# An attention, expert and routing kernel on one core: products of zeros in its opening made float32, fewer in number, and eight of them in other places

## The chip, the cores and the metric

The kernel runs on 1 core of one Trainium2 chip. The metric is the device time in microseconds (us). Times of single runs of the kernel before are 471.6, 471.64 and 473.65 us, with a median of 471.64. One more execution was profiled, and all rows below come from it.

## The reference

```python
for c in range(nc):                                   # chunks of 32 queries
    k_ctx, v_ctx = keys and values from 16 before the chunk to 8 behind it
    k_full, v_full = 8 memory rows, then k_ctx, v_ctx
    a = softmax(q_c @ k_full.T / sqrt(64))            # 4 batches, 8 heads, 768 positions
    out[c] = a @ v_full
x = out as 3072 tokens of 512
h = x @ w_in ; g = h * sigmoid(h) ; y = g @ w_out     # 512 -> 2048 -> 512
logits = y @ phi                                      # 32 slots: 8 experts of 4
slot_input = softmax(logits over tokens).T @ y
slot_out[e] = relu(slot_input[e] @ w1[e]) @ w2[e]     # 512 -> 1024 -> 512
result = softmax(logits over slots) @ slot_out
```

## The kernel before

The 3072 tokens are 24 groups of 128. Attention is done group by group, and the tokens then go through the first two weight matrices in seven blocks of 256 to 512 tokens. The products of a block with one of the 16 pieces of w_in are what the code calls an h.

The program is written out by hand. The string OPENING lists the work of the opening word by word, and each word is one call, put on its engine's queue in that order; every engine then works through its own queue, and waits there for semaphores alone. The first letter says what is done (the dictionary `ops`), the first number for which group or weight piece, and the last numbers of S, T, V and W are PSUM banks:

- q and v load a group's queries with keys, and its values. w and b load a weight piece, c and d convert it in steps (ACT, then DVE), C and D make its high and its low half, R is a small product with phi.
- S is a group's scores (`a_scores`, L266: 32 float32 products), M and U its maximum and subtraction on DVE, E its exponential on ACT, O and N its sum and inverse on DVE, Q its division (Q.1.p: on POOL).
- T turns a group's probabilities (`a_turn`, L311: four 128x128 transposes), A keeps them (ACT, L186), V multiplies them by the values (`a_values`, L328: 32 float32 products), X and Y are the high and the low half of the result (ACT L186, DVE L382).
- h is a group of products with weights (`emit_h`, L399), s and t its tanh and multiplication.
- W is `keep_warm(n, b)`: n products of zeros into bank b (L182), which nothing reads.

The products of zeros are bfloat16, of 128 columns of zeros with 512 others. The zeros lie in a part of the tile `call` that holds results of the routing later on:

```python
warm = [call[:, 0:8].rearrange("p t s -> p (t s)").bitcast(BF16)]       # L114
nc.vector.memset(call[:, 0:8], 0.0)                                     # L755
keep_warm(10)                                                           # L758
```

Ten stand at the start, and 27 in six places of OPENING: W.12.0 ahead of the scores of group 4, W.2.6 ahead of those of group 3, W.3.7 ahead of the values of group 1, W.4.5 ahead of the turn of group 0, W.3.4 ahead of the values of group 0, and W.3.7 ahead of the values of group 3. The order of the groups in the opening is 2, 1, 0, 4, 3 for the scores and 1, 2, 0, 4, 3 for the turns; the values come as 1, 2, 0, 3, 4. After V.4 follow h.0, h.2 and so on, with no more products of zeros in the opening.

The loads are all issued by SP, in the order of their words. A weight piece (512 KB) is loaded into one of five buffers, and so waits until an earlier piece in it has been converted.

Of the kernel before, what the change touches and what calls it, by code (L numbers as in the profile page):

```python
# [11 lines left out]
BF16 = mybir.dt.bfloat16  # L12
# [12 lines left out]


OPENING = """
q.2 q.1 q.0 S.2.4.5 M.2 U.2 w.1 S.1.6.2 c.1.0 i M.1 U.1 E.1 q.4 S.0.3.7 M.0 W.12.0 S.4.1.0 E.2 O.1 N.1 q.3 W.2.6
S.3.4.5 U.0 w.0 c.1.1 O.2 N.2 E.0 O.0 N.0 v.1 c.0.0 c.0.1 v.0 M.4 U.4 Q.1.p T.1.6 A.1.a v.2 Q.2.p T.2.2 A.2.a W.3.7
V.1.3.7 E.4 Q.0.p W.4.5 T.0.6 c.0.3 C.0 D.0.p b.2 X.1 M.3 U.3 E.3 V.2.2.1 w.2 b.0 A.0.a c.2.0 c.2.1 O.4 N.4 W.3.4  # L30
V.0.0.5 v.3 O.3 N.3 X.2 Q.4.p T.4.4 Y.1 Q.3.p X.0 c.2.3 T.3.6 A.3.a W.3.7 V.3.3.7 v.4 A.4.a c.1.3 C.1 D.1.p b.1
V.4.6.4 d.2.0 Y.2 X.3 w.3 Y.0 h.0 h.2 X.4 Y.3 d.1.0 Y.4 s.0 t.0 h.3 z.0 p d.2.1 d.2.3 v.5 d.1.1 d.1.3 s.2 d.0.0 d.0.1
b.3 t.2 z.2 h.1 C.2 D.2.p w.5 d.0.3 R.0 R.1 R.2 s.3 t.3 z.3 h.4 w.4 c.3.0 c.3.1 c.3.3 s.1 t.1 h.5 z.1 C.3 b.5 c.5.0
c.5.1 c.5.3 s.4 t.4 c.4.0 c.4.1 c.4.3 D.3.p h.7 s.5 t.5 z.5 h.6 b.4 d.3.0 d.3.1 d.3.3 R.3 C.4 D.4.v d.5.0 s.7 t.7 s.6
t.6 z.6 q.5 w.6 S.5.2.5 M.5 U.5 C.5 h.9 e.0 D.5.p d.4.0 d.4.1 c.6.0 c.6.1 c.6.3 w.8 s.9 t.9 z.9 h.10 s.10 t.10 q.6
C.6 D.6.v b.7 P.0.3 F.0 d.4.3 d.5.1 d.5.3 h.8 s.8 t.8 d.7.0 d.7.1 h.13 c.8.0 c.8.1 c.8.3 w.7 s.13 t.13 E.5 O.5 h.12
s.12 t.12 z.12 b.6 C.8 z.4 S.6.4.6 w.9 d.7.3 z.7 R.4 R.5 c.7.0 c.9.0 d.6.0 b.8 N.5 h.11 s.11 D.8.p h.16 z.8 z.10 t.11
z.11 d.6.1 d.6.3 w.10 c.7.1 c.7.3 L.0.0 c.9.1 c.9.3 C.7 L.1.0 s.16 t.16 Q.5.p T.5.5 A.5.a R.6 R.7 c.10.0 d.8.0 d.8.1
q.7 M.6 U.6 h.17 s.17 t.17 b.9 e.1 D.7.p h.14 b.10 C.9 d.8.3 s.14 t.14 z.14 E.6 O.6 N.6 w.12 V.5.5.4 v.6 X.5 c.10.1
c.10.3 S.7.6.7 M.7 d.10.0 d.10.1 q.8 h.15 s.15 t.15 z.15 D.9.p h.18 h.19 C.10 D.10.p Y.5 s.18 w.11 z.17 d.9.0 d.9.1  # L40
d.9.3 c.12.0 c.12.1 P.1.4 F.1 d.10.3 b.13 c.12.3 C.12 Q.6.p T.6.5 U.7 A.6.a L.0.1 L.1.1 E.7 R.8 R.9 R.10 D.12.p
V.6.4.6 s.19 t.18 h.20 O.7 N.7 Q.7.p t.19 z.19 h.21 c.11.0 c.11.1 c.11.3 b.11 d.11.0 w.14 s.20 t.20 h.25 C.11 D.11.p
z.13 c.14.0 b.12 d.12.0 s.21 t.21 z.21 h.23 c.14.1 c.14.3 d.11.1 d.11.3 R.11 X.6 T.7.5 Y.6 w.15 s.25 t.25 z.25 d.13.0
d.13.1 d.13.3 e.2 S.8.4.6 M.8 U.8 s.23 t.23 h.22 C.14 P.2.7 v.7 A.7.a V.7.5.4 d.12.1 d.12.3 s.22 t.22 z.22 q.9 E.8
O.8 N.8 F.2 L.1.2 L.0.2 R.12 z.16 D.14.p h.28 s.28 t.28 z.28 h.29 c.15.0 c.15.1 c.15.3 b.14 d.14.0 d.14.1 d.14.3 C.15
D.15.v b.15 d.15.0 d.15.1 d.15.3 h.31 s.29 t.29 z.29 w.13 c.13.0 c.13.1 c.13.3 s.31 Q.8.p t.31 z.31 h.30 v.8 T.8.6
X.7 Y.7 s.30 t.30 z.30 A.8.a R.13 R.14 R.15 e.3 V.8.4.5 v.9 C.13 D.13.v S.9.6.7 q.10 M.9 U.9 X.8 h.24 s.24 t.24 z.24
h.27 s.27 h.26 z.20 z.18 P.3.6 Y.8 t.27 B.0 F.3 L.1.3 z.27 z.23 E.9 O.9 N.9 s.26 t.26 L.0.3 z.26 Q.9.v
"""


# [1 line left out]
def attn_moe_softmoe_kernel(  # L53
# [13 lines left out]
    nc = tc.nc  # L67
    NB = len(BLOCKS)
    L = NB - 1
# [8 lines left out]
    z = const.tile([128, 10240], F32, name="z")  # L78
# [35 lines left out]
    call = const.tile([128, NT, 32], F32, name="call")  # L114
    acc = const.tile([128, 4, 512], F32, name="acc")
    s_run = const.tile([128, 1], F32, name="s_run")
    warm = [call[:, 0:8].rearrange("p t s -> p (t s)").bitcast(BF16)]

    misc = [[4, 5, 6], 0]

    def bank(b, shape, name):
        if b is None:
            return mbank(shape, name)
        return psum.tile(shape, F32, tag=f"b{b}", name=name)

    def mbank(shape, name):
        misc[1] += 1
        return bank(misc[0][misc[1] % len(misc[0])], shape, name)
# [39 lines left out]
    def load_raw(key):  # L168
        o = 7168 if key[0] == "o" else 1024 * (len(raw_t) % 5)
        raw_t[key] = oarena[:, o:o + 1024].bitcast(U32).rearrange("p (n two) -> p n two", two=2)  # L170
        nc.sync.dma_start(out=raw_t[key], in_={"w": win, "b": woutt, "o": wout}[key[0]][key[1]])
# [7 lines left out]
    def keep_warm(n, b=0):  # L179
        pw = bank(b, [128, 512], "ps_warm")  # L180
        for _ in range(n):
            nc.tensor.matmul(pw, warm[0][:, 0:128], warm[0], start=True, stop=True)  # L182

    def copy(eng, out, in_):
        if eng == "a":
            nc.scalar.activation(out=out, in_=in_, func=ACTF.Copy)  # L186
        else:
            nc.vector.tensor_copy(out=out, in_=in_)
# [8 lines left out]
    def conv(key, s):  # L197
        raw = raw_t[key]
        lo_w, hi_w = raw[:, :, 0], raw[:, :, 1]
        if key not in cx:  # L200
            o = (5120, 5632, 6144, 7168, 7680)[len(cx) % 5]
            cx[key] = oarena[:, o:o + 512]
        x = cx[key]
        xb = x.bitcast(U32)
        if s == 0:
            nc.scalar.activation(out=x, in_=hi_w.bitcast(F32), func=ACTF.Prelu, scale=REBIAS, alpha=-(2.0**32))  # L206
        elif s == 1:
            nc.scalar.activation(  # L208
                out=lo_w, in_=raw.bitcast(U16)[:, :, 1], func=ACTF.Copy, scale=2.0**-13, bias=-4095.75 / 8192
            )  # L210
        elif s == 2:
            return
        else:
            nc.vector.scalar_tensor_tensor(  # L214
                out=xb, in0=xb, scalar=3, in1=lo_w, op0=ALU.logical_shift_left, op1=ALU.bitwise_or
            )
# [535 lines left out]
            at(*WO[u], 1, wo_load, u + 1)  # L752

    with tc.manual_schedule():
        nc.vector.memset(call[:, 0:8], 0.0)  # L755
        nc.vector.memset(s_run, 0.0)
        nc.scalar.activation(out=s_run, in_=s_run, func=ACTF.Exp)
        keep_warm(10)  # L758

        def step(fn):  # L760
            return lambda i, *a: fn(i % 2, i // 2, *a)

        ops = {
            "q": load_qk, "v": load_v, "w": lambda f: load_raw(("w", f)), "b": lambda f: load_raw(("b", f)),
            "i": load_cst, "p": load_phi, "W": keep_warm,
            "c": lambda f, s: conv(("w", f), s), "d": lambda f, s: conv(("b", f), s), "C": conv_hi, "D": conv_lo,
            "R": wp_q, "e": wp_keep, "P": wp_sum, "F": wp_out,
            "S": a_scores, "M": a_max, "U": a_sub, "E": a_exp, "O": a_sum, "N": a_inv, "Q": a_norm,
# [48 lines left out]
        last_sum((2, by))  # L817
        c_keep = c_turn(0, 4, bx, "a")
        keep_warm(3, 4)
        last_max()  # L820
        g_turn(L, NF - 1)
# [15 lines left out]
        for tag in ("lp", "ll"):  # L837
            t = sm_p.tile([128, 512], F32, tag=tag, name="siz", bufs=1)
# [46 lines left out]
        for half in range(2):  # L885
            for cb in range(2):
                for m in (2 * half, 2 * half + 1):
                    for q in range(4):
# [3 lines left out]
                            start=(m == 0), stop=(m == 3), tile_position=(0, 32 * q),  # L892
# [235 lines left out]
```

## Time and profile before

| | |
|---|---|
| median of 3 runs | 471.64 us |
| profiled execution, own time | 471.73 us |
| its span, first to last instruction | 470.0 us |
| mean granted TensorE clock | 0.986 |
| PE busy (products) | 450.1 us, 96% |
| PEld busy (weight loads) | 336.5 us, 72% |
| DVE busy | 343.1 us, 73% |
| ACT busy | 187.2 us, 40% |
| POOL busy | 43.9 us, 9% |
| moved by DMA | 93.68 MB, mean 199 GB/s |

Times in the rows are counted from the first instruction. A row of the timeline merges neighbouring instructions of one line and one pair of operands: start, length, engine, line, operation, tiles, shape and number, and in brackets how long the engine had been idle and what ended that. "issue" there is time in which the engine waited for nothing that the profile shows. PE is TensorE's products, PEld its weight loads, SPq the issuing of loads. Some records of products can be missing, so that a run of 12 may show as 11. A row of stretches has the stretch, its length, and for PE, PEld, DVE, ACT and POOL the busy time and the number of instructions; then PEclk, the share of the full TensorE clock that was granted, the share of the DMA engines' time that was used, and GB/s.

### The profile page before, as it was taken

To read this page: it belongs to the slowest core of one execution; us is meant where nothing else is said; L and a number is where in the kernel's file an instruction comes from. 1 tells how busy PE (TensorE), PEld (TensorE's weight loads), DVE (VectorE), ACT (ScalarE), POOL (GpSimd) and SP (SyncE) were. 2 spreads that over 40 slices of the span, in tenths; PEclk is the share of its full clock that TensorE was granted. 3 is DMA by queue.
4 is the path that set the end of the run, shared out by engine and by line. 5 is a ranking of instruction groups with operands and counts; after the bars stand their busy time and mean duration, and the time that the engine had idled before them with its cause. 6 is when DMAs were issued, how large, how long until landed. Compare 5 with 4: busy or idle time off the path is not lost.

```text
span 470.0 us, 14626 instructions
## 1 busy us (share of the span) xinstructions
PE 450.1 (96%) x6395; PEld 336.5 (72%) x6402; DVE 343.1 (73%) x785; ACT 187.2 (40%) x401; POOL 43.9 (9%) x41
## 2 busy tenths in 40 slices
PE   7699999989999999999999999999999999999992
PEld 4489988979776777677776778677787789643642
DVE  4757788867889998889998699987865764551142
ACT  2468878863342234233343243341343222221132
POOL 0422134300000001000110011100100000000000
PEclk9889999999999999999999999999999999999997
DMA  8947688464111225124442244412314999799988
GB/s 323 396 150 278 246 307 317 165 215 146 54 49 54 99 100 188 46 99 146 144 153 83 93 149 147 144 52 75 101 47 144 404 409 384 285 412 406 400 288 277
DMA packets 30336, 93.68 MB, mean 199 GB/s; under 512 B 2880, under 2 KB 9280, under 8 KB 30272
## 3 DMA queue, kind: packets, MB, share of 16 engines
q1 hardware_dynamic: 30272, 92.74, 53.8%
q8 instruction: 50, 0.82, 0.7%
q14 instruction: 14, 0.11, 0.1%
HBM read 86.44 MB, written 6.29 MB: 197 GB/s over the span
## 4 chain that ended last, share of the span: by engine, by line
PE 84%; DVE 5%; DMA 4%; ACT 2%; issue 2%; SPq 0%; DVEq 0%; ACTq 0%
PE ps_h L399 51%; PE ps_a L579 6%; PE ps_l L446 5%; PE ps_s L266 3%; PE ps_o L960 3%; PE ps_x L352 3%; PE ps_e L926 3%; PE ps_x L328 2%; DMA oarena<-in_win_dram 2%; DMA aarena<-in_qk_dram 1%; PE ps_warm L182 1%; PE ps_f L1009 1%; DVE garena L426 1%; DVE oarena L214 1%; PE ps_t L311 1%
## 5 line engine op out<-in xcount | busy, mean ns | idle before, releaser
L399 PE MATMUL ps_h<-x,w 128*128 128x512 f32 (+2 forms) x704 | 151.6, 359 | 1.5 <-ACT w L186 1.1
L399 PEld LDWEIGHTS ps_h<-x,w 128*128 128x128 f32 x704 | 124.0, 188 | 23.4 <-issue 3.1
L399 PE MATMUL ps_h<-x1a,w 128*128 128x512 f32 (+2 forms) x544 | 139.0, 362 | 0.0
L421 ACT ACTIVATE garena<-ps_h 128x512 f32<-128x512 f32 (+3 forms) x113 | 60.0, 532 | 168.6 <-PE ps_h L399 151.1
L399 PEld LDWEIGHTS ps_h<-x1a,w 128*128 128x128 f32 x544 | 98.9, 188 | 20.0 <-issue 5.0
L426 DVE SCALAR_TENSOR_TENSOR garena<-garena,ps_h 128x512 f32<-128x512 f32 (+3 forms) x113 | 67.8, 601 | 43.2 <-ACT garena L421 42.1
L430 DVE STREAM_TRANSPOSE z<-garena 128x512 f32<-128x512 f32 (+2 forms) x112 | 69.4, 628 | 4.2 <-PE ps_a L579 0.9
L191 POOL TENSOR_TENSOR aarena<-aarena,smm 128x512 f32<-128x512 f32 x19 | 22.7, 1193 | 226.1 <-DVE smm L301 226.1
L214 DVE SCALAR_TENSOR_TENSOR oarena<-oarena 128x512 uint32<-128x512 uint32 x46 | 31.1, 690 | 7.1 <-ACT oarena L208 7.0
L206 ACT ACTIVATE oarena<-oarena 128x512 f32<-128x512 f32 x46 | 30.4, 665 | 12.6 <-DMA oarena<-in_win_dram 11.9
L208 ACT ACTIVATE oarena<-oarena 128x512 uint32<-128x512 uint16 x48 | 31.6, 667 | 0.0
L399 PE MATMUL ps_h<-x1b,w 128*128 128x512 f32 x64 | 25.0, 390 | 0.0
L446 PE MATMUL ps_l<-garena,aarena 128*32 128x512 f32 (+2 forms) x216 | 24.7, 544 | 0.0
L579 PE MATMUL ps_a<-z,d 32*32 32x512 f32 x672 | 23.6, 598 | 0.0
L274 DVE TENSOR_REDUCE mx<-ps_s 128x4 f32<-128x256 f32 x48 | 17.8, 411 | 6.2 <-PE ps_s L266 6.1
L191 POOL TENSOR_TENSOR w<-oarena,w 128x512 fp32r<-128x512 f32 x12 | 15.9, 1321 | 52.1 <-ACT w L186 52.1
L266 PE MATMUL ps_s<-aarena 64*32 64x64 f32 x1280 | 17.2, 224 | 1.1 <-DMA aarena<-in_qk_dram 1.1
L579 PEld LDWEIGHTS ps_a<-z,d 32*32 32x32 f32 x672 | 10.6, 103 | 9.6 <-issue 5.9
L293 ACT ACTIVATE aarena<-aarena 128x512 f32<-128x512 f32 x20 | 12.6, 629 | 7.9 <-DVE aarena L290 5.7
L590 DVE SCALAR_TENSOR_TENSOR acc<-acc,al,ps_a 128x512 f32<-128x512 f32 x20 | 13.9, 742 | 2.5 <-PE ps_a L579 2.4
L266 PEld LDWEIGHTS ps_s<-aarena 64*32 64x32 f32 x1280 | 13.9, 105 | 2.5 <-DMA aarena<-in_qk_dram 1.2
L287 DVE TENSOR_TENSOR aarena<-ps_s,mx 128x256 f32<-128x256 f32 x40 | 14.8, 409 | 0.1
(211 smaller groups left out, 469.6 us busy)
## 6 DMA issues: line engine op xcount, KB each, us to landing
aarena<-in_qk_dram SPq DMA_DIRECT2D x20, 608.0 KB, 5.4
aarena<-in_v_dram SPq DMA_DIRECT2D x20, 512.0 KB, 4.1
oarena<-in_win_dram SPq DMA_DIRECT2D x16, 512.0 KB, 5.2
oarena<-in_woutt_dram SPq DMA_DIRECT2D x16, 512.0 KB, 5.7
oarena<-in_wout_dram SPq DMA_DIRECT2D x16, 512.0 KB, 3.2
w<-in_w_dram SPq DMA_DIRECT2D x16, 512.0 KB, 7.1
z<-in_w_dram SPq DMA_DIRECT2D x9, 512.0 KB, 8.0
oarena<-in_w_dram SPq DMA_DIRECT2D x8, 512.0 KB, 9.3
```

Source lines behind the costliest of these rows:

```text
L191: (nc.gpsimd if eng == "p" else nc.vector).tensor_tensor(**kw)
L206: nc.scalar.activation(out=x, in_=hi_w.bitcast(F32), func=ACTF.Prelu, scale=REBIAS, alpha=-(2.0**32))
L208: nc.scalar.activation(out=lo_w, in_=raw.bitcast(U16)[:, :, 1], func=ACTF.Copy, scale=2.0**-13, bias=-4095.75 / 8192)
L214: nc.vector.scalar_tensor_tensor(out=xb, in0=xb, scalar=3, in1=lo_w, op0=ALU.logical_shift_left, op1=ALU.bitwise_or)
L266: nc.tensor.matmul(ps[r][q, p], t[h, p, q], t[h, p, w:w + 64], start=True, stop=True)
L274: nc.vector.tensor_reduce(out=mx[:, 4 * r:4 * r + 4], in_=ps_t[g][r], axis=AX.X, op=ALU.max)
L399: nc.tensor.matmul(ph, w_t[f][:, wi, 128 * c:128 * c + 128], x[c], start=(c == 0 and m == 0), stop=(c == 3 and m == 2),)
L421: nc.scalar.activation(out=g[:, t], in_=h_t[j, f][:, t], func=ACTF.Tanh, scale=0.5)
L426: nc.vector.scalar_tensor_tensor(out=g[:, t], in0=g[:, t], scalar=1.0, in1=h[:, t], op0=ALU.add, op1=ALU.mult)
L430: nc.vector.transpose(out=z_view(j)[:, slot], in_=g_t[j, f])
L446: nc.tensor.matmul(rt[j, "pl"][32 * m:32 * m + 32], wp[:, f], g_t[j, f], start=(k == ks[0]), stop=(k == ks[-1] or j == L and m > 1 and k = ...
L579: nc.tensor.matmul(ps[q][32 * cg:32 * cg + 32], d[p, t], zv[p, :, t], start=(b < 4), stop=(b >= nb - 4), tile_position=(32 * q, 32 * cg),)
```

## The change

A second helper makes products of zeros in float32. The zeros become twice as many (512 float32 columns; the bfloat16 products still use the first 256). Ten bfloat16 products at the start become two float32 and two bfloat16 ones. In OPENING, W.12.0 becomes Z.3.0 in the same place; W.2.6 ahead of the scores of group 3, W.3.7 ahead of the values of group 1, W.4.5 ahead of the turn of group 0 and W.3.4 ahead of the values of group 0 are gone; Z.2.6 stands ahead of the turn of group 1 and Z.3.4 ahead of the values of group 2. W.3.7 ahead of the values of group 3 stays. The table OPENING is otherwise the same, word for word:

```
before: ... M.0 W.12.0 S.4.1.0 ... q.3 W.2.6 S.3.4.5 ... Q.1.p T.1.6 ... W.3.7 V.1.3.7 E.4 Q.0.p W.4.5 T.0.6 ... E.3 V.2.2.1 ... N.4 W.3.4 V.0.0.5
now:    ... M.0 Z.3.0 S.4.1.0 ... q.3 S.3.4.5 ... Q.1.p Z.2.6 T.1.6 ... V.1.3.7 E.4 Q.0.p T.0.6 ... E.3 Z.3.4 V.2.2.1 ... N.4 V.0.0.5
```

```diff
@@ -114,7 +114,8 @@
     call = const.tile([128, NT, 32], F32, name="call")
     acc = const.tile([128, 4, 512], F32, name="acc")
     s_run = const.tile([128, 1], F32, name="s_run")
-    warm = [call[:, 0:8].rearrange("p t s -> p (t s)").bitcast(BF16)]
+    zeros = call[:, 0:16].rearrange("p t s -> p (t s)")
+    warm = [zeros[:, 0:256].bitcast(BF16)]
 
     misc = [[4, 5, 6], 0]
 
@@ -180,6 +181,11 @@
         pw = bank(b, [128, 512], "ps_warm")
         for _ in range(n):
             nc.tensor.matmul(pw, warm[0][:, 0:128], warm[0], start=True, stop=True)
+
+    def zero_products(n, b):
+        pw = bank(b, [128, 512], "ps_warm")
+        for _ in range(n):
+            nc.tensor.matmul(pw, zeros[:, 0:128], zeros, start=True, stop=True)
 
     def copy(eng, out, in_):
         if eng == "a":
@@ -752,17 +758,18 @@
             at(*WO[u], 1, wo_load, u + 1)
 
     with tc.manual_schedule():
-        nc.vector.memset(call[:, 0:8], 0.0)
+        nc.vector.memset(zeros, 0.0)
         nc.vector.memset(s_run, 0.0)
         nc.scalar.activation(out=s_run, in_=s_run, func=ACTF.Exp)
-        keep_warm(10)
+        zero_products(2, 0)
+        keep_warm(2)
 
         def step(fn):
             return lambda i, *a: fn(i % 2, i // 2, *a)
 
         ops = {
             "q": load_qk, "v": load_v, "w": lambda f: load_raw(("w", f)), "b": lambda f: load_raw(("b", f)),
-            "i": load_cst, "p": load_phi, "W": keep_warm,
+            "i": load_cst, "p": load_phi, "Z": zero_products, "W": keep_warm,
             "c": lambda f, s: conv(("w", f), s), "d": lambda f, s: conv(("b", f), s), "C": conv_hi, "D": conv_lo,
             "R": wp_q, "e": wp_keep, "P": wp_sum, "F": wp_out,
             "S": a_scores, "M": a_max, "U": a_sub, "E": a_exp, "O": a_sum, "N": a_inv, "Q": a_norm,
```

On PE, from the scores of group 3 to the values of group 1, the program stood so before (call holds the zeros, ps_s are scores, ps_t turns, ps_x values; "x32" is 32 instructions of the program, and a float32 product is one row with its weight load in it):

```order
L182 LDWEIGHTS call
L182 MATMUL ps_warm<-call 128x512
L182 LDWEIGHTS call
L182 MATMUL ps_warm<-call 128x512
L266 MATMUL ps_s<-z 32x64 x32
L311 MATMUL ps_t<-cst,z 128x128 x8
L182 LDWEIGHTS call
L182 MATMUL ps_warm<-call 128x512
...
L328 MATMUL ps_x<-z 64x32 x32
```

and stands so now:

```order
L272 MATMUL ps_s<-z 32x64 x32
L188 MATMUL ps_warm<-call 128x512 x2
L317 MATMUL ps_t<-cst,z 128x128 x8
L334 MATMUL ps_x<-z 64x32 x32
```

The two bfloat16 products ahead of the scores are gone, two float32 ones stand between the scores and the eight turns of groups 1 and 2, and the values of group 1 follow the turns with nothing between.

On PE, from the values of group 1 to the turn of group 4, the program stood so before:

```order
L328 MATMUL ps_x<-z 64x32 x32
L182 LDWEIGHTS call
L182 MATMUL ps_warm<-call 128x512
...
L311 MATMUL ps_t<-cst,aarena 128x128 x4
L328 MATMUL ps_x<-z 64x32 x32
L182 LDWEIGHTS call
L182 MATMUL ps_warm<-call 128x512
...
L328 MATMUL ps_x<-aarena 64x32 x32
L311 MATMUL ps_t<-cst,w_332 128x128 x4
```

and stands so now:

```order
L334 MATMUL ps_x<-z 64x32 x32
L317 MATMUL ps_t<-cst,aarena 128x128 x4
L188 MATMUL ps_warm<-call 128x512 x3
L334 MATMUL ps_x<-z 64x32 x32
L334 MATMUL ps_x<-aarena 64x32 x32
L317 MATMUL ps_t<-cst,w_315 128x128 x4
```

The four products ahead of the turn of group 0 and the three ahead of its values are gone; three float32 ones stand between that turn and the values of group 2. On the other engines only the memset of the zeros differs, 128x512 for 128x256.

## Rows read from the trace of the kernel before

**Rows 1.** The page: busy time by engine, and the queue of instructions (packets, MB, share).

```profile
PE 450.1 (96%) x6395; PEld 336.5 (72%) x6402; DVE 343.1 (73%) x785; ACT 187.2 (40%) x401; POOL 43.9 (9%) x41
...
q8 instruction: 50, 0.82, 0.7%
```

**Rows 2.** Timeline of PE, from the start to h.0.

```profile
1.19 4.45 PE L182 MATMUL ps_warm<-call 128*128 128x512 bf16 x10 [1.19 <-DVE s_run L756]
...
8.60 0.86 PE L266 MATMUL ps_s<-aarena 64*32 64x64 f32 x64 [1.08 <-DMA aarena<-in_qk_dram]
...
9.39 2.76 PE L182 MATMUL ps_warm<-call 128*128 128x512 bf16 x11
...
13.12 0.78 PE L266 MATMUL ps_s<-acc 64*32 64x64 f32 x55 [0.60 <-issue]
...
15.15 0.98 PE L311 MATMUL ps_t<-cst,z 128*128 128x128 f32 x7
...
19.17 0.33 PE L311 MATMUL ps_t<-cst,z 128*128 128x128 f32 x1 [3.04 <-issue]
...
20.21 2.06 PE L328 MATMUL ps_x<-z 64*64 64x32 f32 x64
...
30.33 1.15 PE L328 MATMUL ps_x<-z 64*64 64x32 f32 x64
...
32.34 0.38 PE L399 MATMUL ps_h<-x,w 128*128 128x256 f32 x1
```

**Rows 3.** DMA by queue: 10.7-10.9, 16.7-16.8, 22.8-23, 26.4-26.6, 33.6-34.6 us.

```profile
q8 instruction: 1, 0.02, 33.3%
...
q1 hardware_dynamic: 12, 0.04, 103.6%
...
q8 instruction: 1, 0.02, 68.2%
...
q8 instruction: 1, 0.02, 32.1%
...
q8 instruction: 1, 0.02, 27.4%
...
q8 instruction: 1, 0.02, 5.9%
```

**Rows 4.** Three stretches: busy time of each engine, granted clock, DMA share.

```profile
19.00:20.00 1.00, 0.78 (x3) 0.35 (x4) 0.00 (x0) 0.47 (x1) 0.00 (x0) 0.94 1.02 406
20.00:25.00 5.00, 4.78 (x77) 3.38 (x80) 3.31 (x8) 2.37 (x7) 2.46 (x3) 0.50 0.69 271
26.00:27.00 1.00, 0.84 (x33) 0.82 (x31) 0.28 (x1) 0.83 (x3) 0.00 (x0) 0.64 0.05 16
```

**Rows 5.** Chain of waits around the end of h.0: start, us, what.

```profile
34.08 0.40 ACT garena L421
```

**Rows 6.** PE's groups by form: zero products in bfloat16, float32 products (mean ns).

```profile
L182 PE MATMUL ps_warm<-cst 128*128 128x512 bf16 x2 | 0.6, 379 | 0.1
...
L487 PE MATMUL ps_r<-lp,cst 128*128 128x256 f32 x2 | 0.6, 378 | 0.0
```

**Rows 7.** Timeline of DVE, ACT and SP in the opening.

```profile
0.86 0.27 DVE L755 MEMSET call<- 128x256 f32 x1 [0.86 <-PEq L1117]
...
18.00 0.74 DVE L287 TENSOR_TENSOR z<-ps_s,mx 128x256 f32<-128x256 f32 x2
...
22.30 0.66 ACT L186 ACTIVATE x<-ps_x 128x256 fp32r<-128x256 f32 x2 [1.13 <-PE ps_x L328]
...
24.98 0.60 ACT L186 ACTIVATE aarena<-ps_t 128x512 f32<-128x512 f32 x1 [1.50 <-PE ps_t L311]
...
26.72 1.29 DVE L214 SCALAR_TENSOR_TENSOR oarena<-oarena 128x512 uint32<-128x512 uint32 x2 [1.39 <-ACT oarena L208]
...
28.09 0.33 SPq L171 DMA_DIRECT2D oarena<-in_woutt_dram  x1
...
29.68 0.60 ACT L186 ACTIVATE z<-ps_t 128x512 f32<-128x512 f32 x1 [0.35 <-PE ps_t L311]
```

More of the change, by code (lines that the diff above doesn't have):

```diff
@@ L27 @@
 OPENING = """
[L28 to L47, printed above, removed]
@@ L48 @@
-h.27 s.27 h.26 z.20 z.18 P.3.6 Y.8 t.27 B.0 F.3 L.1.3 z.27 z.23 E.9 O.9 N.9 s.26 t.26 L.0.3 z.26 Q.9.v
+q.2 q.1 q.0 S.2.4.5 M.2 U.2 w.1 S.1.6.2 c.1.0 i M.1 U.1 E.1 q.4 S.0.3.7 M.0 Z.3.0 S.4.1.0 E.2 O.1 N.1 q.3 S.3.4.5 U.0
+w.0 c.1.1 O.2 N.2 E.0 O.0 N.0 v.1 c.0.0 c.0.1 v.0 M.4 U.4 Q.1.p Z.2.6 T.1.6 A.1.a v.2 Q.2.p T.2.2 A.2.a V.1.3.7 E.4
+Q.0.p T.0.6 c.0.3 C.0 D.0.p b.2 X.1 M.3 U.3 E.3 Z.3.4 V.2.2.1 w.2 b.0 A.0.a c.2.0 c.2.1 O.4 N.4 V.0.0.5 v.3 O.3 N.3
+X.2 Q.4.p T.4.4 Y.1 Q.3.p X.0 c.2.3 T.3.6 A.3.a W.3.7 V.3.3.7 v.4 A.4.a c.1.3 C.1 D.1.p b.1 V.4.6.4 d.2.0 Y.2 X.3 w.3
@@ new lines @@
+Y.0 h.0 h.2 X.4 Y.3 d.1.0 Y.4 s.0 t.0 h.3 z.0 p d.2.1 d.2.3 v.5 d.1.1 d.1.3 s.2 d.0.0 d.0.1 b.3 t.2 z.2 h.1 C.2 D.2.p
+w.5 d.0.3 R.0 R.1 R.2 s.3 t.3 z.3 h.4 w.4 c.3.0 c.3.1 c.3.3 s.1 t.1 h.5 z.1 C.3 b.5 c.5.0 c.5.1 c.5.3 s.4 t.4 c.4.0
+c.4.1 c.4.3 D.3.p h.7 s.5 t.5 z.5 h.6 b.4 d.3.0 d.3.1 d.3.3 R.3 C.4 D.4.v d.5.0 s.7 t.7 s.6 t.6 z.6 q.5 w.6 S.5.2.5
+M.5 U.5 C.5 h.9 e.0 D.5.p d.4.0 d.4.1 c.6.0 c.6.1 c.6.3 w.8 s.9 t.9 z.9 h.10 s.10 t.10 q.6 C.6 D.6.v b.7 P.0.3 F.0
+d.4.3 d.5.1 d.5.3 h.8 s.8 t.8 d.7.0 d.7.1 h.13 c.8.0 c.8.1 c.8.3 w.7 s.13 t.13 E.5 O.5 h.12 s.12 t.12 z.12 b.6 C.8
@@ new lines @@
+z.4 S.6.4.6 w.9 d.7.3 z.7 R.4 R.5 c.7.0 c.9.0 d.6.0 b.8 N.5 h.11 s.11 D.8.p h.16 z.8 z.10 t.11 z.11 d.6.1 d.6.3 w.10
+c.7.1 c.7.3 L.0.0 c.9.1 c.9.3 C.7 L.1.0 s.16 t.16 Q.5.p T.5.5 A.5.a R.6 R.7 c.10.0 d.8.0 d.8.1 q.7 M.6 U.6 h.17 s.17
+t.17 b.9 e.1 D.7.p h.14 b.10 C.9 d.8.3 s.14 t.14 z.14 E.6 O.6 N.6 w.12 V.5.5.4 v.6 X.5 c.10.1 c.10.3 S.7.6.7 M.7
+d.10.0 d.10.1 q.8 h.15 s.15 t.15 z.15 D.9.p h.18 h.19 C.10 D.10.p Y.5 s.18 w.11 z.17 d.9.0 d.9.1 d.9.3 c.12.0 c.12.1
+P.1.4 F.1 d.10.3 b.13 c.12.3 C.12 Q.6.p T.6.5 U.7 A.6.a L.0.1 L.1.1 E.7 R.8 R.9 R.10 D.12.p V.6.4.6 s.19 t.18 h.20
@@ new lines @@
+O.7 N.7 Q.7.p t.19 z.19 h.21 c.11.0 c.11.1 c.11.3 b.11 d.11.0 w.14 s.20 t.20 h.25 C.11 D.11.p z.13 c.14.0 b.12 d.12.0
+s.21 t.21 z.21 h.23 c.14.1 c.14.3 d.11.1 d.11.3 R.11 X.6 T.7.5 Y.6 w.15 s.25 t.25 z.25 d.13.0 d.13.1 d.13.3 e.2
+S.8.4.6 M.8 U.8 s.23 t.23 h.22 C.14 P.2.7 v.7 A.7.a V.7.5.4 d.12.1 d.12.3 s.22 t.22 z.22 q.9 E.8 O.8 N.8 F.2 L.1.2
+L.0.2 R.12 z.16 D.14.p h.28 s.28 t.28 z.28 h.29 c.15.0 c.15.1 c.15.3 b.14 d.14.0 d.14.1 d.14.3 C.15 D.15.v b.15
+d.15.0 d.15.1 d.15.3 h.31 s.29 t.29 z.29 w.13 c.13.0 c.13.1 c.13.3 s.31 Q.8.p t.31 z.31 h.30 v.8 T.8.6 X.7 Y.7 s.30
@@ L49 @@
+t.30 z.30 A.8.a R.13 R.14 R.15 e.3 V.8.4.5 v.9 C.13 D.13.v S.9.6.7 q.10 M.9 U.9 X.8 h.24 s.24 t.24 z.24 h.27 s.27
+h.26 z.20 z.18 P.3.6 Y.8 t.27 B.0 F.3 L.1.3 z.27 z.23 E.9 O.9 N.9 s.26 t.26 L.0.3 z.26 Q.9.v
 """
```

## The prediction

> **What bounds the kernel now.** TensorE does: it is busy for 450.1 of 470.0 us [rows 1], so what counts is where it stands still or runs slowly. The timeline of PE up to its first dense stretch, h.0 at 32.34 [rows 2], shows two gaps that end on "issue", which is no other engine and no load: 0.60 us in the scores of group 4, and 3.04 us ahead of the very last of the eight turns T.1 and T.2. T.2's other three had gone, so its operands were there.
>
> I read these gaps as PE's own instructions arriving late. Queue q8 moved 0.82 MB in 50 packets, some 16 KB each, and PE has 6395 products and 6402 weight loads: 256 instructions to a packet [rows 1]. At the first gap 55 of 64 products were left, at the second one turn of eight [rows 2]. A float32 product is a load and a product twice over, a bfloat16 product or a turn once; so up to the first gap there are 22 zero products (44), three groups of scores (384) and 19 instructions of the fourth, 447; up to the second, 24 zero products (48), five groups (640) and seven turns (14), 702. The difference is 255: one block. So the ends of blocks lie at 447, 703, 959 and 1215.
>
> The DMA view by queue in short stretches gives the packets: they start near 10.8, 16.75, 22.9, 26.5 and 33.6 [rows 3], and take 0.682 x 0.1 x 16 = 1.09 us. PE goes on at 13.12 and 19.17 [rows 2], each time 1.3 us after such a packet's end. A packet starts 3.6 to 3.8 us after PE has begun the block before it (13.12 to 16.75, 19.17 to 22.9) while the data queue fills the engines, 103.6% by the view [rows 3], and at once at 26.5, where it carries nothing. So while inputs stream, a block takes some 6.05 us, and PE cannot have the fourth before 19.17 + 6.05 = 25.2.
>
> The second gap costs more than itself: the granted clock goes from full to half (2.4 to 1.2 GHz) at about 19.88 and back at 26.72 [rows 4], having stood through the 1.08 and 0.60 us gaps. At half clock V.1 takes 2.06 us; V.3 and V.4 take 32.34 - 30.33 = 2.01 together at full clock, 0.0157 us a product [rows 2].
>
> **What a gain at h.0 is worth.** Behind h.0 the chain goes on to its tanh on ACT at 34.08 [rows 5], and each later weight load is issued when a buffer comes free. Nothing there hangs on absolute time, so I carry h.0's shift to the end unchanged.
>
> **The change part by part.** A full-width float32 product of 256 columns lasts 378 ns, a bfloat16 one of 512 columns 379 [rows 6]; so a float32 product of zeros of 512 columns is two such products of double length: as long as four bfloat16 ones, in 4 instructions for 8. At full clock twelve took 2.76 us, 0.23 each; the first ten 4.45, 0.43 each, which is the half-clock rate [rows 2].
>
> *Start:* 2 float32 and 2 bfloat16 for ten: the same time. The memset is twice as long, +0.27 us [rows 7], hidden by the 1.08 us wait for group 0's load at 8.60 [rows 2]. Cost 0; without that cover 0.27.
>
> *Ahead of S.4:* three for twelve, the same time. The block's end now lies 447 - 408 = 39 instructions into S.4 instead of 19. PE still goes on at 13.12. Cost 0.
>
> *Two ahead of S.3 go, two float32 ahead of T.1 come:* S.4 ends near 13.8, S.3 (0.86) at 14.7 if its load is in, two products (8 x 0.23) at 16.5, eight turns (0.14 each) at 17.6. The second end, 703, is now 15 instructions into V.1. A.1 is done 0.6 after T.1, at 17.7; V.1 does 7 of 64 by 17.8 and waits until 19.17: 1.4 us idle for 3.04. The gap ends where it ended; what it leaves undone is 57 products (0.9) instead of a turn, three zero products and all of V.1.
>
> *The clock:* 1.4 us idle is near the 1.08 that it stood through and well under the 3.04 after which it fell, so I take full clock from 19.17. The Trainium skill, page "TensorE: Matmul & The Clock Gate", Part 4 (PE-mode transpose), says that transposes do not count towards the full clock as other products do; by that the eight turns in the middle help little and the clock falls as before (the second rival). No row here separates turns from products.
>
> *V.1 to V.4:* V.1 ends at 20.1; T.0 20.7; three float32 products (12 x 0.23, into a bank that DVE leaves at 18.74 [rows 7]) 23.4; V.2 reaches the third end, 959, after 61 products at 24.4 and waits until 25.2. So these products cost nothing here: fetching ends last. V.2 is done at 25.25, V.0 26.3, T.4 and T.3 27.4, A.3 (0.60 [rows 7]) 28.0, with the three bfloat16 products beside it. V.3 starts at 28.0 for 30.33 and reaches the fourth end, 1215, after 50 products at 28.8.
>
> *The fourth end is the unknown.* Its packet is asked for at 25.2. With idle DMA it starts at once, as at 26.5: there by 27.9, no wait, h.0 at 30.0, gain 2.3. Under load, as from V.3's start of a block near 30.9 to 33.6 [rows 3], it needs 2.7 + 1.1 + 1.3: there at 30.3, a wait of 1.5, gain 0.8; with the 3.7 of the full queue the gain is nil. Which? ACT goes from X.1 at 22.30 to c.2.1, on which DVE's two conversions (1.29) follow at 26.72, 1.5 us of it waiting for T.0; then SP issues the next weight load at 28.09 [rows 7]. With X.1 at 20.1 and T.0 already done, c.2.1 ends near 23.1 and that load goes out near 24.5, just ahead of 25.2. I take one and a half loads of 512 KB at 406 GB/s [rows 4] ahead of the packet, 2 us: there at 29.6 to 29.8, a wait of 1.0, **h.0 at 31.0, a gain of 1.3 us**.
>
> Sum: 471.73 (the profiled execution, 470.0 of it span) - 1.3 = 470.4, or 470.3 against the median of 471.64, which stands 0.09 lower. Bounds of this case: 469.4 (no second wait) to 471.8 (3.7 us and a little).
>
> The Trainium skill, page "Runtime: NRT & Kernel Launch", section "Instruction fetch mechanics", has blocks of 256 instructions, as counted above, but says that the prefetch hides them. By that, fewer instructions bring nothing and the eight extra products are pure cost (the fourth rival); the trace disagrees, with 1.3 us from packet to product twice.
>
> **Rivals.** *No second wait:* the next loads go out after 25.2. For: ACT and DVE queues often slip by some tenths. Against: my sum has them 0.7 us earlier. 469.4. Chance 0.17.
>
> *The clock falls as before, at 19.9 to 26.7:* V.1 ends 20.3, T.0 21.4, the three products now take 12 x 0.43 = 5.1 until 26.5, V.2 27.6, h.0 at 32.4 as before. 471.8. For: half of the old idle time is still there, and turns and values use small parts of the array. Chance 0.15.
>
> *The clock falls later (slower):* the waits at 24.4 and 28.8 come on top of the first, and the fall lands on h.0 and its successors, which are dense. A low stretch of 6.84 us costs 3.4 there, less the gain of 1.3 or nothing: 473.8 to 475.1. It decides from the point where the waits inside V.2 and V.3 reach some 2 us each. Against: each is short. Chance 0.09.
>
> *The instructions are not the cause:* the 3.04 us belong to that turn and stay, and 45 units of products instead of 37 add 8 x 0.23 = 1.8: 473.5. Against: the count of 255. Chance 0.07.
>
> **How the numbers follow.** The forecast has 0.52. What a measurement tells from no change is about 0.5%, 2.36 us, so faster means under 469.28. The no-wait rival lies on that line: half of its 0.17, and 0.08 of the forecast for terms that I set too high: 0.17. Slower, over 474.0: most of the late fall and a little of the last rival: 0.09. Between: 0.74. The range of 469.2 to 472.4 takes in the forecast's bounds and two rivals, and leaves out the late fall and the last one, 0.16, and a little at the lower end.
>
> **What would show it.** Right: the gap ahead of T.2's last turn is gone, one of about 1.4 us stands after V.1's seventh product and ends at 19.2; the packets near 10.8, 16.8 and 22.9 stay; granted clock 1.00 from 20 to 27; a short gap near the end of V.2 until 25.2, one after V.3's fiftieth product; h.0 near 31.0. Wrong: packets at other times, half clock after 20, or h.0 earlier than 30.0 or later than 32.4; or a shift at h.0 that is gone by the end.

## The result, and the profile after

The changed kernel takes 475.19 us (median of 20 runs, 472.48 to 478.45), the kernel before 471.7 us on the same chip (20 runs, 470.54 to 475.59). The ratio is 1.0072, with a 95% interval of 1.0054 to 1.0089: slower by 0.7%, where 470.3 and no change that can be told were forecast, with a range up to 472.4. The profiled execution of the changed kernel took 472.48 us and is the fastest of its 20, so its rows show the smallest loss; the first experiment profiles the same kernel in an execution of 476.49 us. (Of the float32 products in the opening, five stand in other places, Z.2.6 and Z.3.4, and not the eight of the title; three stand where W.12.0 stood.)

The page after, for [rows 1], and the group of the h products with the waits ahead of them, in all and by what ended most of them:

```profile
PE 450.1 (96%) x6390; PEld 335.2 (71%) x6390; DVE 343.9 (73%) x785; ACT 187.7 (40%) x401; POOL 43.9 (9%) x41
...
q8 instruction: 50, 0.82, 0.7%
...
L405 PE MATMUL ps_h<-x,w 128*128 128x512 f32 (+2 forms) x704 | 151.9, 360 | 3.0 <-issue 1.6
```

PE does as much as before. What is new stands behind the last bar: ahead of those h products PE now waits 3.0 us in all, 1.6 of it on "issue". Before, the same group had this line:

```profile
L399 PE MATMUL ps_h<-x,w 128*128 128x512 f32 (+2 forms) x704 | 151.6, 359 | 1.5 <-ACT w L186 1.1
```

The timeline of PE in the opening, for [rows 2]; L188 are the float32 products of zeros, L272 scores, L317 turns, L334 values:

```profile
13.09 0.69 PE L272 MATMUL ps_s<-acc 64*32 64x64 f32 x45 [1.20 <-issue]
...
18.01 0.31 PE L334 MATMUL ps_x<-z 64*64 64x32 f32 x6 [0.25 <-ACT z L192]
19.29 1.11 PE L334 MATMUL ps_x<-z 64*64 64x32 f32 x58 [0.97 <-issue]
...
20.83 2.74 PE L188 MATMUL ps_warm<-call 128*128 128x512 f32 x6
23.50 1.11 PE L334 MATMUL ps_x<-z 64*64 64x32 f32 x59
25.46 0.31 PE L334 MATMUL ps_x<-z 64*64 64x32 f32 x5 [0.85 <-issue]
...
28.43 0.91 PE L334 MATMUL ps_x<-z 64*64 64x32 f32 x46
30.10 0.48 PE L334 MATMUL ps_x<-z 64*64 64x32 f32 x18 [0.76 <-issue]
...
31.44 0.39 PE L405 MATMUL ps_h<-x,w 128*128 128x256 f32 x1
```

The 3.04 us gap ahead of T.2's last turn is gone. In its place stand three short ones, inside V.1, V.2 and V.3, and h.0 starts 0.90 us earlier (32.34 to 31.44). (The text ahead of the prediction says that an engine waits in its queue "for semaphores alone"; that is so of the program, but these gaps are waits for the instructions themselves.) The packets of the instruction queue, for [rows 3], by queue in the stretches 16.8-16.9, 27.8-28 and 70.3-70.4 us (a packet starts inside each):

```profile
q8 instruction: 1, 0.02, 68.4%
...
q8 instruction: 1, 0.02, 27.5%
...
q8 instruction: 1, 0.02, 60.7%
```

The one for V.1 starts where it did (the next one too, in 22.8-23); the one for V.3 starts at 27.8, because SP had issued the next weight load at 25.20 ([rows 7]: 28.09 before), just ahead of the moment at which PE went on in V.2 (the experiment with late loads below tests that "because"):

```profile
25.20 0.33 SPq L172 DMA_DIRECT2D oarena<-in_woutt_dram  x1
```

The granted clock, for [rows 4], in a stretch of the opening and in one around a later gap (columns as there): full in both.

```profile
20.00:25.00 5.00, 4.62 (x94) 2.75 (x87) 4.34 (x9) 2.79 (x6) 2.92 (x3) 1.00 0.68 267
...
72.00:74.00 2.00, 1.22 (x7) 1.22 (x8) 0.98 (x3) 0.49 (x1) 0.00 (x0) 1.00 0.70 216
```

Now to the place where the gain is lost. The timeline of PE after, from the values of group 5 (V.5) over the scores of group 7 (S.7) to the values of group 6 (V.6):

```profile
68.74 1.14 PE L334 MATMUL ps_x<-aarena 64*64 64x32 f32 x64
69.81 0.86 PE L272 MATMUL ps_s<-aarena 64*32 64x64 f32 x64
70.59 0.62 PE L405 MATMUL ps_h<-x,w 128*128 128x384 f32 x2
72.78 1.49 PE L405 MATMUL ps_h<-x,w 128*128 128x384 f32 x7 [1.57 <-issue]
...
81.48 1.13 PE L334 MATMUL ps_x<-aarena 64*64 64x32 f32 x64
```

and before:

```profile
70.32 1.14 PE L328 MATMUL ps_x<-aarena 64*64 64x32 f32 x64
71.38 0.86 PE L266 MATMUL ps_s<-aarena 64*32 64x64 f32 x64
72.17 2.01 PE L399 MATMUL ps_h<-x,w 128*128 128x384 f32 x10
...
81.21 1.14 PE L328 MATMUL ps_x<-aarena 64*64 64x32 f32 x64
```

At V.5 the changed kernel is 1.58 us ahead (70.32 - 68.74), at V.6 0.27 behind: 1.85 us lost between them, by one gap that ends on "issue". The row counts 1.57 us of it as idle; by the starts, products of this h are 0.18 us apart, so the third was due near 70.95 and came 1.83 us later. The end of the span is 0.7 behind (470.7 against 470.0); the half microsecond more comes in two small steps, near 90 and near 449 us. So 40 us after the last word that the change touches, a new gap takes back the whole gain.

**Where that gap comes from.** It is the end of a block again. In program order, with all of PE's instructions counted (products, weight loads and the waits for semaphores, which the prediction's count left out), the gaps of the opening lie at 449, 705, 961 and 1217, each within two instructions; 449 + 8 x 256 = 2497 lies on the second row of h behind S.7, where PE stands. The change leaves 22 fewer instructions on PE from V.0 on (24 fewer of zero products, two more waits for semaphores), so every later end moves 22 instructions on in the work. V.5 and S.7 are 256 instructions together, a whole block, and PE goes through them in 1.14 + 0.86 us. Before, the end fell 22 instructions earlier, inside S.7, and the packet for what follows had started at 67.69, 2.6 us ahead of V.5's start; after, it started at 70.35, 1.6 us behind it, and took 0.97; 1.46 later PE went on.

### The profile page after: what moved, and what is told of

It reads as the page before. It is cut to its first block, busy times and chain, and to the rows that moved or that the text cites. A ratio compares the mean times of both kernels' runs of the same rounds, so it can differ in the third digit from the quotient of the medians.

```text
span 470.7 us, 14611 instructions
## 1 busy us (share of the span) xinstructions
PE 450.1 (96%) x6390; PEld 335.2 (71%) x6390; DVE 343.9 (73%) x785; ACT 187.7 (40%) x401; POOL 43.9 (9%) x41
## 4 chain that ended last, share of the span: by engine, by line
PE 81%; DVE 6%; DMA 6%; issue 3%; ACT 2%; SPq 0%; DVEq 0%; ACTq 0%
PE ps_h L405 48%; PE ps_a L585 6%; PE ps_l L452 4%; PE ps_s L272 3%; PE ps_o L967 3%; PE ps_x L358 3%; PE ps_e L933 3%; DMA oarena<-in_win_dram 3%; PE ps_x L334 2%; PE ps_warm L188 2%; DVE oarena L220 2%; DMA oarena<-in_woutt_dram 1%; DMA aarena<-in_qk_dram 1%; DVE garena L432 1%; PE ps_f L1016 1%
## 5 line engine op out<-in xcount | busy, mean ns | idle before, releaser
L272 PE MATMUL ps_s<-aarena 64*32 64x64 f32 x1280 | 17.2, 224 | 0.3 <-DMA aarena<-in_qk_dram 0.3
L272 PEld LDWEIGHTS ps_s<-aarena 64*32 64x32 f32 x1280 | 13.9, 105 | 1.7 <-DMA aarena<-in_qk_dram 0.5
```

Source lines behind the costliest of these rows:

```text
L272: nc.tensor.matmul(ps[r][q, p], t[h, p, q], t[h, p, w:w + 64], start=True, stop=True)
```

## Experiments

Two theories. **A:** every one of these gaps on "issue" is the end of a block, and what the change costs is the place of the ninth end (2497) and of the fourth (1217). **B:** the products of zeros themselves cost it: float32 ones hold the clock worse, or too few are left. All runs were timed in five rounds against the kernel before, whose medians were 471.96, 471.76 and 471.66 in the three sets. The padding used below is products of 32 weights by 8 columns into a bank that nobody reads.

### The changed kernel again

No edit.

> The changed kernel itself once more, for another profile and the granted clock of each execution. Theory A (ends of instruction blocks): the gap of 1.6 us two products behind the scores of group 7, near 72.8 us, is there again, and in the slower executions the clock falls once more, after that gap, onto dense products: mean clock near 0.99, span near 473.4. Rival B (the earlier loads collide later with other work): no gap on issue near 72.8 in another execution, the loss is a wait for a load or an engine. Rival C: the clock falls in the opening after all, in most executions, with 0.50 between 20 and 30 us. Time 475 in either case, 473 to 477.

475.36 us (472.24 to 476.49, 12 runs), ratio 1.0062 [1.0040, 1.0083]. Its profiled execution took 476.49 us. The timeline of PE in the opening and around V.5:

```profile
21.14 4.44 PE L188 MATMUL ps_warm<-call 128*128 128x512 f32 x6
...
31.86 0.48 PE L334 MATMUL ps_x<-z 64*64 64x32 f32 x18 [1.67 <-issue]
...
33.20 0.39 PE L405 MATMUL ps_h<-x,w 128*128 128x256 f32 x1
...
71.33 1.14 PE L334 MATMUL ps_x<-aarena 64*64 64x32 f32 x64
...
75.37 3.39 PE L405 MATMUL ps_h<-x,w 128*128 128x384 f32 x11 [1.57 <-issue]
...
85.52 1.13 PE L334 MATMUL ps_x<-aarena 64*64 64x32 f32 x64
```

and the stretches behind that gap (the last but two columns is the granted clock):

```profile
75.00:76.00 1.00, 0.63 (x3) 0.63 (x4) 0.53 (x2) 0.04 (x1) 0.00 (x0) 0.93 0.68 228
76.00:79.00 3.00, 3.00 (x12) 3.00 (x12) 0.00 (x0) 0.42 (x2) 0.00 (x0) 0.50 0.89 320
79.00:80.00 1.00, 1.00 (x9) 1.00 (x9) 0.86 (x2) 0.60 (x2) 0.32 (x1) 0.87 0.98 388
```

PE does all of V.5, S.7 and two rows of h, and then stands, as in the first profile; but here the clock goes to half behind it, for some 3.4 us, on dense h products. From V.5 to V.6 this execution loses 3.30 us against before (71.33 - 70.32 = +1.01, 85.52 - 81.21 = +4.31): 1.83 for the gap, as in the first profile, which leaves some 1.5 for the clock. In the opening it is also slower than the first profile: three zero products take 4.44 us for 2.74, at half clock for part of them, and V.3 waits 1.67; h.0 is at 33.20, 0.86 later than before. So the opening's gain is not steady either, from +0.90 to -0.86 in two executions.

### Eleven tiny products ahead of V.3, so that later ends lie where they did

```diff
-... A.3.a W.3.7 V.3.3.7 v.4 ...
+... A.3.a W.3.7 K.11.7 V.3.3.7 v.4 ...
```

> The changed kernel with 11 tiny products (8 columns, a weight load of 32) behind the three bfloat16 products ahead of V.3: 22 instructions more, so that from there on the blocks of 256 end where they ended before the change. Theory A: no gap near 72.8, the shift of -1.3 to -1.6 us that stands at 60 us is carried to the end: span of the profile 468.4 to 469.2, median 470.0 to 471.5, at least 3 us under the changed kernel. Rival B: the gap or the loss stays, 474 to 476.

472.66 us (470.04 to 474.86, 12 runs), ratio 1.0004 [0.9981, 1.0027]. PE's timeline, ahead of h.0 and behind V.5:

```profile
30.93 0.60 PE L339 MATMUL ps_x<-z 64*64 64x32 f32 x27 [1.56 <-issue]
...
69.94 1.14 PE L339 MATMUL ps_x<-aarena 64*64 64x32 f32 x64
...
71.79 2.47 PE L410 MATMUL ps_h<-x,w 128*128 128x384 f32 x13
```

22 instructions of padding, which are work and nothing else, make the kernel 2.5 to 2.7 us faster than the changed one; A had expected at least 3, and a median of at most 471.5. The gap behind S.7 is gone: thirteen rows of h in one piece. B has no place for that. The wait in V.3 stays, 1.56 us, and keeps part of what A had expected.

### Float32 in place, no product moved

The kernel before with three runs of bfloat16 zero products made float32 where they stand (24 instructions fewer).

```diff
-... M.0 W.12.0 S.4.1.0 ... Q.0.p W.4.5 T.0.6 ...
+... M.0 Z.3.0 S.4.1.0 ... Q.0.p Z.1.5 T.0.6 ...
-        keep_warm(10)
+        zero_products(2, 0)
+        keep_warm(2)
```

> The kernel before with its products of zeros turned to float32 in place and none moved: 10 into 2 and 2, W.12 into 3, W.4.5 into 1; 24 instructions fewer by the values of group 1, the same array time. Theory A: block ends move as in the change, so a gap of some 1.5 us near 72 comes although nothing was moved; in the opening the long gap no longer stands ahead of T.2's last turn but in the three products or V.1 behind it, and still ends at 19.2. The clock falls near 20 as before. 473 to 475. Rival B: no gap near 72, time as before, 471 to 472.

473.5 us (472.43 to 477.08, 12 runs), ratio 1.0042 [1.0017, 1.0067]. PE's timeline behind S.7, and the stretch after it by windows:

```profile
70.58 0.80 PE L405 MATMUL ps_h<-x,w 128*128 128x384 f32 x3
73.04 1.22 PE L405 MATMUL ps_h<-x,w 128*128 128x384 f32 x4 [1.67 <-issue]
```

```profile
74.00:77.00 3.00, 3.00 (x13) 3.00 (x13) 0.55 (x1) 1.01 (x2) 0.01 (x1) 0.50 0.97 349
```

With other zero products in other places, but about as many instructions fewer, the same gap stands almost at the same place of the work, with half clock behind it: behind three products of h, where the change has two.

### Fewer products in bfloat16, no float32

```diff
-... Q.0.p W.4.5 T.0.6 ... N.4 W.3.4 V.0.0.5 ... A.3.a W.3.7 V.3.3.7 ...
+... Q.0.p T.0.6 ... N.4 V.0.0.5 ... A.3.a V.3.3.7 ...
```

> The kernel before without its last ten bfloat16 products but three (W.4.5, W.3.4 and the W.3.7 ahead of V.3 left out): the opening is as before up to 20.2 us, with 20 instructions fewer behind it. Theory A: a gap of 1 to 2 us near 72 and 472.5 to 474.5, though nothing ahead of 20 us differs. Rival B: no gap, and 0.5 us less or the same as before, 471 to 472.

478.24 us (477.52 to 478.98, 6 runs), ratio 1.0125 [1.0100, 1.0150]. PE's timeline behind S.7, and stretches of the opening with the granted clock:

```profile
74.39 0.44 PE L399 MATMUL ps_h<-x,w 128*128 128x384 f32 x1
76.73 1.73 PE L399 MATMUL ps_h<-x,w 128*128 128x384 f32 x7 [1.90 <-issue]
```

```profile
20.00:36.00 16.00, 14.63 (x338) 13.57 (x333) 8.28 (x18) 8.76 (x21) 4.63 (x4) 0.50 0.51 190
36.00:37.00 1.00, 1.00 (x8) 1.00 (x7) 0.32 (x1) 0.74 (x2) 0.00 (x0) 0.58 0.00 0
```

The gap behind S.7 comes without one float32 product, so it is the count and not the type. It even moves as the count says: with waits for semaphores counted, 20, 22 and 24 instructions are missing ahead of this h here, in the change and in the kernel with float32 in place, and the gap stands behind one, two and three products of it, which is instruction 2498 in program order in all three. But there is a second cost, which is B's, and by it the median lies 3.7 us over the 474.5 that A had allowed: with these ten products gone, the clock that falls near 19.8 comes back only behind 36, where it came back at 26.7 before [rows 4]. All six executions have a mean clock of 0.969 to 0.972, against 0.986 in the profile of before. So the products of zeros that stand behind the 3 us gap shorten the half clock there.

### The same padding behind the opening

The changed kernel with its opening untouched, and the eleven tiny products near 40 us, between dense h products.

```diff
-... R.0 R.1 R.2 s.3 ...
+... R.0 R.1 R.2 K.11.5 s.3 ...
```

> The changed kernel with 11 tiny products (22 instructions) behind R.2, near 40 us, so that the opening is the changed kernel's to the letter and the blocks end where they ended before the change only from there on. Theory A: no gap near 72.8 us, no fall of the clock near 74 to 77, 3 us under the changed kernel: median 471.5 to 473 (with 0.4 us for the products themselves if nothing hides them); what is left above 470 is the opening's own. Rival B: a gap on issue of over 1 us is still there between 68 and 80 us, 474 to 476.

473.05 us (470.91 to 473.73, 12 runs), ratio 1.0016 [0.9997, 1.0035]. PE's timeline:

```profile
30.28 0.48 PE L339 MATMUL ps_x<-z 64*64 64x32 f32 x18 [1.03 <-issue]
...
71.34 2.47 PE L410 MATMUL ps_h<-x,w 128*128 128x384 f32 x13
```

The gap is gone, and 2.1 to 2.3 us of the loss with it (3 had been expected). The profiled execution, the fastest of the twelve, keeps the opening's gain to the end of the span (469.1 against 470.0); the median does not.

### The block's end left where it is, S.7 taken out of it

The changed kernel with S.7 behind the next h; no product added or removed, one wait for a semaphore fewer.

```diff
-... c.10.3 S.7.6.7 M.7 d.10.0 d.10.1 q.8 h.15 ...
+... c.10.3 d.10.0 d.10.1 h.15 S.7.6.7 M.7 q.8 ...
```

> The changed kernel with the scores of group 7 moved from behind the values of group 5 to behind h.15: not one instruction more or less, and the ends of blocks stay where they are; but the block that was used up in 1.9 us by values and scores now has twelve dense products in it and lasts some 3.5 us. Theory A: the gap near 72.8 shrinks from 1.6 to between 0 and 0.7 us, 2 to 3 us under the changed kernel where the clock then holds: median 471.5 to 473.5. Rival B: no change, 474 to 476.

472.66 us (471.40 to 474.01, 11 runs), ratio 1.0017 [1.0001, 1.0034]. PE's timeline:

```profile
74.15 0.78 PE L272 MATMUL ps_s<-aarena 64*32 64x64 f32 x54
75.30 0.32 PE L272 MATMUL ps_s<-aarena 64*32 64x64 f32 x10 [0.37 <-issue]
```

The packet is as late as in the changed kernel (73.08, 2.3 us behind V.5's start), yet only 0.37 us of idle is left, now inside S.7, where instruction 2497 has come to lie: with twelve products of h between V.5 and S.7 the block in front of the end lasts longer. That is the other half of A: the end costs what the block in front of it is too short to cover.

### The fourth end as well: next weight loads behind the packet

The changed kernel with the padding near 40 us, and with one weight piece's conversion behind V.4 and Y.2, so that SP issues the loads that wait for it later.

```diff
-... v.4 A.4.a c.1.3 C.1 D.1.p b.1 V.4.6.4 d.2.0 Y.2 X.3 ...
+... v.4 A.4.a V.4.6.4 Y.2 c.1.3 C.1 D.1.p b.1 d.2.0 X.3 ...
```

> As pad40, and c.1.3 (with C.1, D.1, b.1) moved on DVE's queue behind the low half of group 2's result, Y.2, so that the next weight loads are issued near 27 us instead of 25.2. Theory on the fourth end of a block: its packet, asked for near 25.4 us, now finds idle DMA and starts at once, not 2.4 to 4 us later; the wait inside V.3 (0.8, 1.8 and 1.6 us in three profiles) is gone and h.0 starts near 30.7. Median 470 to 471.2, 1 to 2 us under pad40. Rival: the packet comes late whatever is loaded, V.3 waits as before, time as pad40 or, if the loads are then missed, slower.

**470.16 us** (469.29 to 471.50, 10 runs), ratio 0.9972 [0.9959, 0.9986]: faster than both kernels. SP's issue and PE's timeline:

```profile
27.39 0.33 SPq L172 DMA_DIRECT2D oarena<-in_woutt_dram  x1
```

```profile
28.17 1.15 PE L339 MATMUL ps_x<-z 64*64 64x32 f32 x64
...
30.18 0.38 PE L410 MATMUL ps_h<-x,w 128*128 128x256 f32 x1
...
79.27 1.14 PE L339 MATMUL ps_x<-aarena 64*64 64x32 f32 x64
```

With the load at 27.39 instead of 25.20, the packet starts at 26.35 instead of 27.83, V.3 goes through in one piece, and h.0 stands at 30.18, 2.16 ahead of before; at V.6 it is still 1.94 ahead.

### Float32 in place, with padding

The kernel with float32 in place, and twelve tiny products behind R.2.

```diff
-... R.0 R.1 R.2 s.3 ...
+... R.0 R.1 R.2 K.12.5 s.3 ...
```

> The kernel before with float32 products in place (f32only) and 12 tiny products, 24 instructions, behind R.2. Theory A: the gap of 2 us near 73 and the fall behind it are gone, 3 us or so under f32only: median 470 to 471.5, 0 to 0.3% under the kernel before. Rival B: 473 to 474.

471.49 us (470.45 to 474.18, 11 runs), ratio 0.9993 [0.9976, 1.0011], 2.0 us under the same kernel without padding. Behind S.7 thirteen rows of h run in one piece here too:

```profile
73.95 2.47 PE L410 MATMUL ps_h<-x,w 128*128 128x384 f32 x13
```

(This profiled execution, 473.68 us, is the second slowest of its eleven: V.2 waits 2.40 us, and the clock stands at half from about 25.3 to 32.1.)

### The late loads without padding, and in the kernel before

The edit of the loads alone, first on the changed kernel and then on the kernel before:

```diff
-... A.4.a c.1.3 C.1 D.1.p b.1 V.4.6.4 d.2.0 Y.2 X.3 ...
+... A.4.a V.4.6.4 Y.2 c.1.3 C.1 D.1.p b.1 d.2.0 X.3 ...
```

(The first of the two texts calls the padding forty products; it is the eleven near 40 us.)

> The change with the next weight loads moved behind Y.2 as in the run before with that move, but without the forty products of padding... that is, PE's instructions stand where the changed kernel has them, so the block's end at 2497 lies again behind the values of group 5 with the scores of group 7 next. Theory A (each gap is the end of a block of 256 PE instructions, and its place is what decides): the wait in V.3 is gone (h.0 near 30.2, a shift of about -2.2 against before at 40 us), and the gap of 1.5 to 2.0 us near 71 us is back, often with a stretch of half clock behind it: shift near -2.2 up to 70 us, -0.5 to +1.5 behind 75; median 471.5 to 473, 1.5 to 2.5 us over the version with padding. Rival (the late loads are what gains, the padding gives nothing): no gap near 71, median near 470.2.

473.43 us (471.53 to 476.24, 12 runs), ratio 1.0038 [1.0018, 1.0057]: 3.3 us over the version with padding. PE's timeline:

```profile
69.94 1.14 PE L334 MATMUL ps_x<-aarena 64*64 64x32 f32 x64
...
74.45 2.93 PE L405 MATMUL ps_h<-x,w 128*128 128x384 f32 x11 [2.04 <-issue]
...
84.62 1.13 PE L334 MATMUL ps_x<-aarena 64*64 64x32 f32 x64
```

From 0.38 ahead at V.5 to 3.41 behind at V.6: the gap is back, and half clock behind it (0.50 from 76 to 78 us). V.3 has no wait, as expected; h.0 is at 31.28 and not near 30.2, since in this execution the zero products of the opening ran partly at half clock; the median lies a little over the 473 that had been allowed.

> The kernel before with the next weight loads moved behind Y.2, products of zeros as they were. Theory A: before has no wait in V.3, since its packet near 26.5 us starts at once with the loads at 28.1 behind it; the move has nothing to take away, so 471.7 within 0.5 us, ratio 0.999 to 1.001, and the 3.0 us gap ahead of the last turn stands. Rival (the move gains by itself, whatever the products of zeros are): 470.2 or so, ratio 0.997, which would make the change itself worth nothing in the best version.

471.92 us (470.40 to 474.88, 12 runs), ratio 1.0006 [0.9988, 1.0025]. The 3 us gap stands (3.11). Later loads are worth nothing by themselves, and the change needs both the padding and the later loads to gain. Padding and later loads together in the kernel before, without the change, were not tried.

## Why the prediction was wrong

**Bound and cause of the gaps: right.** Late blocks of 256 instructions were the reading, and the gaps on "issue" of 0.37 us and more in the first 80 us of twelve profiles all lie at multiples of 256 from the first, within two instructions. The forecast's 447, 703, 959 and 1215 leave out the waits for semaphores and the first instructions of the program: three ahead of the first end before, eleven ahead of V.3 after the change. That is why V.3 stopped after 46 products and not after 50.

**Opening: right within half a microsecond in the first profile, but for one load (0.7).** Forecast, and then measured in the first profile: the gap in V.1 after 7 of 64, after 6; PE on again at 19.17, at 19.29; packets near 16.75 and 22.9, the same; V.2's wait to 25.2, to 25.46; the next load issued at 24.5, at 25.20, ahead of V.3's packet as feared; V.3's wait 1.0, 0.76; h.0 at 31.0, at 31.44. The gain was 0.9 for 1.3. The start cost nothing and the clock stayed full in that execution. In three of six further profiles with the same zero products (again, S.7 apart, late loads without padding) the clock fell on the three ahead of V.2, near 21 us, at a cost of up to 1.7 us; the second rival had a fall in the opening, longer and at another price. (Its reason that turns use a small part of the array is not in the rows: they are 128*128.) In those three V.1 had waited 1.24 to 1.26 us, in the four that kept full clock 0.42 to 0.97; that the wait decides it is not shown. But the prediction's step from the 1.08 us that the clock stood through to the 1.4 forecast for V.1 did not hold there, and the full clock of the first profile, with V.1 waiting 0.97, is in part luck.

**The step that failed** is "Nothing there hangs on absolute time, so I carry h.0's shift to the end unchanged." Behind h.0 nothing hangs on absolute time, but something hangs on the count of instructions. The prediction itself had counted 39 - 19 = 20 instructions by which the first ends move, and stopped counting at h.0. All later ends move as well, and the ninth moves to where 256 instructions last only 2 us and its packet comes late: 0.90 us ahead at h.0 and 1.58 at V.5 become 0.27 behind at V.6. The prediction's own last sign of being wrong, a shift at h.0 that is gone by the end, is what came. Four comparisons in which little but this end differs price it: padding near 40 us 2.1 to 2.3 us (473.05 against 475.19 and 475.36), S.7 apart 2.5 to 2.7, padding under float32 in place 2.0, padding under the late loads 3.3.

**The clock behind it.** The third rival had a later fall on dense h products, and 473.8 to 475.1. Such a fall does come, but behind the gap at 2497 (1.57 us idle in the execution that shows it) and not behind the waits in V.2 and V.3, and it costs some 1.5 us and not 3.4. That its time is near the measured one is a sum of other terms: 1.8 of gap, 1.5 of clock in part of the executions, and an opening that gains less than it did in the first profile. How often the clock falls can be told from its mean, which is on record for every execution. Of the seven profiles with the changed opening, the four without a fall between 10 and 460 us have a mean of 0.993 to 0.996, the three with one or two falls 0.986 to 0.989. Of the changed kernel's 20 executions, four at 0.993 to 0.996 took 472.48 to 473.17 us, the other sixteen, at 0.983 to 0.990, 474.73 to 478.45. So where no fall is likely the change is 0.8 to 1.5 us slower than the median of before, and the rest of the median's 3.5 goes with the clock; where it fell in the executions that were not profiled is not shown.

**Fewer instructions as the means.** By the Trainium skill, "Runtime: NRT & Kernel Launch", "Instruction fetch mechanics", prefetch mostly hides the fetching of blocks; here ends cost 0.4 to 3.1 us each, wherever the block in front was short or its packet stood behind loads. The fourth rival's term, extra products as pure cost, did not show: padded, and with later loads, the change is faster than before (470.16 against 471.76).

**Left open.** Why the padded versions with the change's opening stay 0.7 to 1.3 us over before in their medians. With padding near 40 us it goes with the clock: four executions at 0.993 to 0.995 took 470.91 to 471.78 us, eight at 0.989 to 0.991 472.80 to 473.73. A fall in the opening, as in three of the profiles, is the likely cause, but the slower ones were not profiled. And why the ninth packet starts 4 to 5 us later, measured from V.5, for 22 instructions: eleven products of the h ahead of V.5 are at most some 1.7 us of it (an estimate; its 24 take 3.7). For the rest, SP issues weight loads in that stretch (at 65.04 and 65.93 after, at 66.61 and 67.51 before), and a request that comes just behind them would wait for them, as V.3's did; that this is so there was not tried by itself.

## What to carry to other kernels

On TensorE, adding or removing instructions moved every later block end, so the count has to be followed through the whole program and not only through the stage that is edited: look for the places where small products use up 256 instructions in about 2 us while loads stream, and keep ends away from them. A few tiny instructions move the ends at will (22 of them were worth 2 to 3 us here), and loads that are issued just ahead of a packet's request are better issued behind it (with that, V.3's wait of 0.8 to 1.7 us was gone). A shift that is won early should be checked at several later landmarks, since one page's total hides a gain and a loss.

## What the runs showed of the hardware

- Eleven products that do nothing made the kernel 2 to 3 us faster, by a gap that went 30 to 40 us behind the place where they stand.
- With 20, 22 and 24 instructions fewer, the same gap stood behind one, two and three products of one h: an end of a block is fixed to the instruction.
- The same gap (1.57 us by the rows of both executions of the changed kernel) was followed by full clock in one and by some 3.4 us of half clock in the other, though the products around it were the same.
- With the zero products behind the 3 us gap taken out, values, turns and the first h products together left the clock at half from 20 to 36 us (0.50), for 6.8 us before.
